# Prologue evictions regrouped by engine, a weight cast and a weight copy moved between engines, and one block's convolution placed one product later

## The chip, the cores and the metric

The kernel runs on one core of a Trainium2 chip. The metric is the device time of one execution in microseconds (us); for a kernel it is the median of several runs. A profiled execution, taken apart from these runs, gives the trace. Engines are named as in the profile: PE is TensorE (matmuls; PEld are its weight loads), DVE is VectorE, ACT is ScalarE, POOL is GpSimd, SP is SyncE, which here only issues DMAs.

## What is computed

The reference, cut to its two parts. `x` is 8 x 3904 x 192, `weight` 8 x 7; `moe_w1` and `moe_w2` are 192 x 1024, `moe_w3` 1024 x 1024, `moe_w_out` 1024 x 192, all float32.

```python
def _attn_ref(x, weight):
    w = softmax(weight, axis=-1)              # 8 heads, 7 taps
    x_pad = np.concatenate([np.zeros((B, 6, D)), x], axis=1)
    idx = np.arange(S)[:, None] + np.arange(7)[None, :]
    x_unf = x_pad[:, idx, :].reshape(B, S, 7, H, D // H)
    return np.einsum('hk,bskhg->bshg', w, x_unf).reshape(B, S, D)

def _moe_ref(x, w1, w2, w3, w_out):           # x: 31232 x 192, from _attn_ref
    a = x @ w1
    b = x @ w2
    return ((a * b) @ w3) @ w_out
```

A causal depthwise convolution of seven taps, a gate that multiplies two products, and two further products.

## The kernel before

**Two streams, rounds and blocks.** The 31232 tokens are two streams of 15616, side by side (`NS` = 2, index `r`). A round `R` is 512 tokens of both streams; there are 31 rounds, worked in groups of four (`GROUP`). The convolution works in windows of 64 rows that give 58 tokens each (`ST`), and windows are gathered in blocks: `SIZES` is 6, 4, 8, 10, 8 and then six blocks of 36 and one of 20. Blocks 0 to 4 make rounds 0 to 3, block 5 makes rounds 4 to 7, and so on.

**Convolution.** `conv` multiplies the windows of x (`xb`, bf16, loaded by POOL's DMAs) with banded 64x64 matrices (`Aband`, made from the taps in the prologue), some heads at a time, into one pair of PSUM banks; the results are evicted to `convo`. One eviction of four heads is two instructions, since the 192 features are stored in three parts of 64 (`NP` = 3, index `k`) and 96 features span one part and a half.

**Transposition to xT.** The products need features on the partitions: `xT[k]`, 64 features of stream 0 over 64 of stream 1, a ring of 2048 tokens. For blocks 0 to 4 TensorE transposes `convo` into PSUM (`pe_transpose`, `joint_transposes`), and an engine evicts it to `xT`. From block 5 on SP stores `convo` to `rows` in DRAM (`store`) and brings it back with transposing DMAs (`transposes`, called by `send`, three for each round). SP's DMAs run in the order in which they are written; a transpose waits for the stores of its rows.

**First product.** For each round and each of eight column tiles `ft` of 128: six matmuls with w1 (three `k`, two streams, 512 columns, the two streams on the upper and lower half of the array) into one pair of banks, six with w2 into another; ScalarE casts the first pair to bf16 (`asb`), VectorE multiplies it with the second into `abT`. Weights lie in `wd[0]` and `wd[1]`, twice each: partitions 0 to 63 for stream 0 and a copy on 64 to 127 for stream 1. They come in four quarters of 256 columns. The first quarter is loaded as float32 (`wfirst`) and cast by four instructions (`cast_w(i, r, engine)`); the others are loaded by POOL with the cast in the DMA (`load_w`) onto the lower half, and copied to the upper half by `copy_w(part, i, engine)`.

**Second product.** `W_sb` is w3 times w_out, made once (`w3_product`) from w3 transposed by DMAs (`w3_transposes`). `second_product(R, r)` multiplies 512 tokens of `abT` with it and sends the output; in the first group POOL issues these outputs, later SP.

**PSUM pairs.** There are four pairs of banks. `banks()` takes the next free one from a list, `drained(p)` puts it back at the end; what a matmul really waits for are the reads of the pair that it gets.

**Order of the work.** The order on each engine is that of the program text (a manual schedule). Prologue: bands and casts, block 0 (L526 to L531), block 1 (L532, L535), the first two column tiles of round 0 in two parts, 348 tokens from block 0 (L534, L536) and 164 from block 1 (L537), then the other six tiles. `first_product` takes a dictionary `between` of what follows a given tile. After rounds 0 to 3 and `w3_product` come the eight second products of the first group; with `at` the convolutions of block 5 (three thirds: heads 0 to 2, 3 to 5, 6 and 7) are placed behind the products 0, 1 and 2, and those of block 6 behind 4, 5 and 6. Block 5's last third is followed by its stores, and `send(7)` sends rounds 4 to 7 to `xT`. Then rounds 4 to 7 are worked, and so on.

Of the kernel before, what the change touches and what calls it, by code (L numbers as in the profile page):

```python
# [16 lines left out]
def kernel(  # L17
# [53 lines left out]
    def banks():  # L71
        p = free.pop(0)
        return p, pairs[:, NS * p:NS * p + NS, :]
# [4 lines left out]
    def drained(p):  # L78
        assert p not in free
        free.append(p)  # L80
# [107 lines left out]
    def cast_w(i, r, f):  # L188
        f(out=wd[i][Q * r:Q * r + Q, :, 0:WC[1]], in_=wfirst[:, i])

    def copy_w(part, i, f):
        cs = slice(WC[part], WC[part + 1])
        f(out=wd[i][Q:128, :, cs], in_=wd[i][0:Q, :, cs])  # L193

    load_w(1)
    cast_w(1, 1, nc.gpsimd.tensor_copy)
    load_w(2)
    load_x(2, between=[seq((copy_w, 1, i, nc.gpsimd.tensor_copy) for i in range(2))])
    load_w(3)
    for i in range(2):  # L200
        copy_w(2, i, nc.gpsimd.tensor_copy)
    load_x(3)

    def warm(n):
# [70 lines left out]
    def conv(b, h0, nh, evict=None):  # L275
        n = SIZES[b] // 2
        if h0 == 0:
            convo_of[b] = work.tile([128, n, NP, NS, Q], BF16, tag="convo", bufs=2, name="convo")
        convo = convo_of[b]
        p, cps = banks()  # L280
        wd = nh * G

        def view(ps, r):
            return cps[ps, r, 0:n * wd].rearrange("p (w g) -> p w g", g=wd)

        for j in range(nh):
            h = h0 + j
            for c in range(2):
                xb, w0 = xb_of[b][c]
                for r in range(NS):  # L290
                    nc.tensor.matmul(  # L291
                        view(slice(Q * c, Q * c + Q), r)[:, :, j * G:(j + 1) * G],
                        band_of(h, r),
                        xb[Q * r:Q * r + Q, w0:w0 + n, h * G:(h + 1) * G],
                        start=True, stop=True)
        src = cps[:, :, 0:n * wd].rearrange("p r (w g) -> p r w g", g=wd)
        o, moves = 0, []
        for k, c0, m in segments(h0 * G, wd):
            moves.append((convo[:, :, k, :, c0:c0 + m].rearrange("p w r g -> p r w g"),
                          src[:, :, :, o:o + m]))  # L300
            o += m
        if h0 + nh == H:
            del xb_of[b]
        if evict == ():
            return p, moves
        if evict == "streams":
            assert nh == H
            return p, [(convo[:, :, :, r, :], src[:, r].rearrange("p w (k g) -> p w k g", k=NP))
                       for r in range(NS)]
        for e, (dst, part) in enumerate(moves):  # L310
            f = evict or [nc.scalar.copy]
            f[e % len(f)](out=dst, in_=part)  # L312
        drained(p)
# [57 lines left out]
    def width(R):  # L371
        return min(CH, TS - R * CH)

    def first_part(R, ft, c0, c1, ks=tuple(range(NP))):
        ab = abT_of[R]
        r0 = (R * CH) % RING
        pq = []
        for i in range(2):
            q, p = banks()
            pq.append((q, p))  # L380
            for k in ks:
                for r in range(NS):
                    rs = slice(Q * r, Q * r + Q)
                    nc.tensor.matmul(  # L384
                        p[:, r, c0:c1], wd[i][rs, k, ft * 128:(ft + 1) * 128],
                        xT[k][rs, r0 + c0:r0 + c1],
                        start=(k == ks[0]), stop=(k == ks[-1]))
        (qa, pa), (qb, pb) = pq
        asb = work.tile([128, NS, CH], BF16, tag="asb", bufs=3, name="asb")
        nc.scalar.copy(out=asb[:, :, c0:c1], in_=pa[:, :, c0:c1])  # L390
        nc.vector.tensor_tensor(out=ab[:, ft, :, c0:c1], in0=asb[:, :, c0:c1],  # L391
                                in1=pb[:, :, c0:c1], op=ALU.mult)
        drained(qa)
        drained(qb)

    def first_rest(R, fts, c0, c1):
        ab = abT_of[R]
        r0 = (R * CH) % RING
        n, ne = c1 - c0, len(fts)
        assert ne * n <= CH  # L400
        pq = []
        for i in range(2):
            q, p = banks()
            pq.append((q, p))
            for e, ft in enumerate(fts):
                for k in range(NP):
                    for r in range(NS):
                        rs = slice(Q * r, Q * r + Q)
                        nc.tensor.matmul(  # L409
                            p[:, r, e * n:e * n + n], wd[i][rs, k, ft * 128:(ft + 1) * 128],  # L410
                            xT[k][rs, r0 + c0:r0 + c1], start=(k == 0), stop=(k == NP - 1))
        (qa, pa), (qb, pb) = pq
        asb = work.tile([128, NS, CH], BF16, tag="asb", bufs=3, name="asb")
        nc.scalar.copy(out=asb[:, :, 0:ne * n], in_=pa[:, :, 0:ne * n])
        a, b = (t[:, :, 0:ne * n].rearrange("p r (e c) -> p r e c", e=ne) for t in (asb, pb))
        nc.vector.tensor_tensor(
            out=ab[:, fts[0]:fts[0] + ne, :, c0:c1].rearrange("p e r c -> p r e c"),
            in0=a, in1=b, op=ALU.mult)
        drained(qa)
        drained(qb)  # L420

    def first_tile(R):
        abT_of[R] = work.tile([128, JT, NS, CH], BF16, tag="abT", bufs=GROUP, name="abT")
# [1 line left out]
    def first_product(R, between=None, fts=range(JT)):  # L425
        if R not in abT_of:
            first_tile(R)
        for ft in fts:
            first_part(R, ft, 0, width(R))
            if between and ft in between:  # L430
                between[ft]()

# [66 lines left out]
    made = [band(1, 0), band(1, 1)]  # L499
    put(V, *made[0])  # L500
    put(V, *made[1])
    cast_w(1, 0, A)

    def move_all(p, moves, fs):
        for f, m in zip(fs, moves):
            move(f, m)
        drained(p)

    def joint_transposes(b):
        n = SIZES[b] // 2  # L510
        assert n * NP <= 2 * CH // 64
        convo = convo_of[b]
        p, tps = banks()
        tps = bf16(tps)
        t0, moves = tok(FIRST[b]), []
        for k in range(NP):
            for w in range(n):
                nc.tensor.transpose(
                    out=tps[:, k * n + w, :],
                    in_=convo[:, w, k].rearrange("p r g -> p (r g)"), identity=ident)  # L520
            src = tps[:, k * n:k * n + n, :].rearrange("p w (c s) -> p c w s", c=2)
            moves.append((xT[k][:, t0:t0 + 2 * n * ST].rearrange("p (c w s) -> p c w s", c=2, w=n),
                          src[:, :, :, 0:ST]))
        return p, moves

    move_all(*conv(0, 0, 4, ()), (V, A))  # L526
    move_all(*conv(0, 4, 4, ()), (A, V))
    for k, f in ((0, A), (2, V), (1, V)):
        p, *m = pe_transpose(0, k)
        move(f, m)  # L530
        drained(p)  # L531
    move_all(*conv(1, 0, H, "streams"), (A, V))  # L532
    first_tile(0)
    first_part(0, 0, 0, EARLY, (0, 2, 1))  # L534
    move_all(*joint_transposes(1), (A, A, V))  # L535
    first_part(0, 1, 0, EARLY)  # L536
    first_rest(0, range(2), EARLY, CH)  # L537
    load_w3(0)
    for i in range(2):
        copy_w(3, i, P)  # L540
# [4 lines left out]
    def need(R):  # L545
        return next(i for i in range(NWIN) if tok(i) >= (R + 1) * CH)

    def send(last):
# [2 lines left out]
            sent[0] += 1  # L551

    first_product(0, {
        4: seq([(conv, 2, 0, 4)]),
        5: seq([(conv, 2, 4, 4)]),
        6: seq([(pe_transposes, 2)]),
# [33 lines left out]
    for p, rounds in enumerate(groups):  # L590
        b = PROLOGUE_BLOCKS + p
        order = rounds[-1:] + rounds[:-1] if rounds[-1] == NR - 1 else rounds
        for j, R in enumerate(order if p else ()):
            first_product(R)
            send(R + GROUP)
            if j < 2 and b < NB:
                P(out=pace, in_=abT_of[R][0:1, JT - 1, 1, 0:2])  # L597
                load_x(b, (j,))
        if b < NB:
            zero(b)  # L600
        at = {1: [(b, slots[0])], 3: [(b, slots[1])], 5: [(b, slots[2])]}
        if p == 0:
            at = {0: [(5, slots[0], (V, A))], 1: [(5, slots[1], (V, A))],
                  2: [(5, slots[2], (V, A), need(GROUP))], 4: at[1], 5: at[3], 6: at[5]}
        for i, (R, r) in enumerate((R, r) for R in rounds for r in range(NS)):
            second_product(R, r, R == NR - 1 and r == 1, nc.sync if p else nc.gpsimd)
            for c in at.get(i, ()) if b < NB else ():
                conv_heads(*c)
            if p == 0 and i == 2:
                send(2 * GROUP - 1)  # L610
    assert sent[0] == NR

# [29 lines left out]
```

## Time and profile before

| what | value |
|---|---|
| median of 3 runs | 524.01 us (523.96 to 524.15) |
| profiled execution, its own time | 523.71 us |
| its span, first to last instruction | 522.0 us |
| mean granted TensorE clock | 0.998 |
| TensorE busy | 514.2 us, 98% of the span |
| VectorE, ScalarE busy | 358.1 us, 326.1 us |
| GpSimd busy | 58.6 us |

The time of the profiled execution is 1.7 us above its span, which lies outside the instructions. A row of the timeline gives the start from the beginning of the span, the duration from the first to the last of a run of like instructions, the engine, the line of the kernel, the operation, output and inputs, the shapes, their number, and in brackets the idle time of the engine before it with what ended it. A q behind an engine's name marks DMA issues. In the table of waits the three numbers are the time in all, the count and the longest. In the chain that ended last each piece has its start, its length and its engine, tile and line.

### The profile page before, as it was taken

How to read it: one execution, taken by the hardware profiler on the slowest of the kernel's cores; microseconds unless marked ns; L12 is line 12 of the kernel's file. 1: busy time of each engine (PE TensorE's matmuls, PEld its weight loads, DVE VectorE, ACT ScalarE, POOL GpSimd, SP SyncE). 2: the span in 40 equal slices, each digit the busy share in tenths (PEclk: the TensorE clock that was granted, in tenths of full speed). 3: DMA queues.
4: the chain of work that ended last, by engine and by line, in shares of the span. 5: the costliest groups of instructions: out<-in, count | busy, mean ns of one | idle time of the engine just before them, and what ended most of it. 6: DMA issues, size and time to landing. Idle time of an engine off the chain costs nothing.

```text
span 522.0 us, 13021 instructions
## 1 busy us (share of the span) xinstructions
PE 514.2 (98%) x5576; PEld 340.5 (65%) x5576; DVE 358.1 (69%) x347; ACT 326.1 (62%) x414; POOL 58.6 (11%) x98
## 2 busy tenths in 40 slices
PE   7999999999999999999999999999999999999997
PEld 4555788444894558845588455884558845599567
DVE  6778646799538995389953899438993299912870
ACT  6887642777437774377743777337774377735762
POOL 8601622030000200003000020001200000000000
PEclk9999999999999999999999999999999999999999
DMA  8979998699556973569645698456824532034004
GB/s 115 157 145 125 148 225 219 161 209 147 129 156 164 111 99 102 152 165 124 86 110 148 158 126 84 118 146 156 102 45 122 153 96 31 17 104 140 1 3 151
DMA packets 133420, 64.61 MB, mean 124 GB/s; under 512 B 90304, under 2 KB 132642, under 8 KB 133298
## 3 DMA queue, kind: packets, MB, share of 16 engines
q1 hardware_dynamic: 94320, 44.06, 35.0%
q0 software_dynamic: 38896, 19.62, 28.8%
q8 instruction: 43, 0.70, 0.6%
q14 instruction: 15, 0.12, 0.1%
q10 hardware_dynamic: 146, 0.10, 0.1%
HBM read 33.25 MB, written 36.52 MB: 134 GB/s over the span
## 4 chain that ended last, share of the span: by engine, by line
PE 90%; issue 3%; DMA 2%; DVE 2%; ACT 1%; POOL 1%; ACTq 0%; POOLq 0%; DVEq 0%
PE pairs L384 56%; PE pairs L445 31%; PE pairs L291 3%; DMA xb<-in_x_dram 2%; DVE abT L391 1%; ACT asb L390 1%; PE pairs L207 1%; POOL xb L120 0%; DVE cprod L248 0%; PE pairs L344 0%; ACT convo L312 0%; DVE convo L489 0%; POOL rows L335 0%; POOL wo_b L567 0%; PE pairs L409 0%
## 5 line engine op out<-in xcount | busy, mean ns | idle before, releaser
L391 DVE TENSOR_TENSOR abT<-asb,pairs 128x1024 bf16<-128x1024 bf16 (+2 forms) x248 | 297.9, 1201 | 76.8 <-ACT asb L390 39.9
L384 PE MATMUL pairs<-xT,wd 64*128 64x512 bf16 (+2 forms) x2976 | 319.4, 372 | 0.8 <-DVE abT L391 0.3
L390 ACT CAST asb<-pairs 128x1024 bf16<-128x1024 f32 (+2 forms) x248 | 247.1, 996 | 67.4 <-PE pairs L384 66.7
L384 PEld LDWEIGHTS <-wd 64*128 64x128 bf16 x2976 | 162.2, 94 | 151.4 <-issue 2.3
L445 PE MATMUL pairs<-W_sb,abT 128*128 128x192 bf16 x1952 | 166.1, 246 | 0.0
L445 PEld LDWEIGHTS <-abT 128*128 128x128 bf16 x1952 | 159.6, 98 | 9.7 <-issue 9.7
L450 ACT COPY osb<-pairs 128x384 f32<-128x384 f32 x122 | 58.3, 478 | 116.0 <-PE pairs L445 116.0
L312 DVE CAST convo<-pairs 128x864 bf16<-128x864 f32 (+5 forms) x67 | 50.8, 815 | 68.5 <-PE pairs L291 64.3
L120 POOL DMA_DIRECT2D xb<-in_x_dram x42 | 32.2, 782 | 6.4 <-PE pairs L384 3.7
L597 POOL COPY pace<-abT 1x2 bf16<-1x2 bf16 x10 | 1.8, 176 | 239.6 <-DVE abT L391 239.6
L291 PE MATMUL pairs<-xb,Aband 64*64 64x432 bf16 (+5 forms) x384 | 17.7, 284 | 0.5 <-POOL xb L575 0.5
L291 PEld LDWEIGHTS <-Aband 64*64 64x64 bf16 x384 | 7.2, 106 | 7.8 <-issue 6.6
L312 ACT CAST convo<-pairs 128x512 bf16<-128x512 f32 (+4 forms) x15 | 8.1, 584 | 1.3 <-PE pairs L291 1.2
L457 POOL DMA_DIRECT2D out_dram<-osb x8 | 6.1, 759 | 18.4 <-ACT osb L450 18.0
L450 DVE COPY osb<-pairs 128x192 f32<-128x192 f32 x1 | 0.4, 357 | 11.1 <-PE pairs L445 11.1
L480 PEld LDWEIGHTS <-w3T 128*128 128x128 bf16 x64 | 5.2, 98 | 0.4 <-issue 0.4
L480 PE MATMUL pairs<-wo_b,w3T 128*128 128x192 bf16 x64 | 5.5, 246 | 0.0
L344 PE MATMUL pairs<-ident,convo 128*128 128x128 bf16 x48 | 3.9, 219 | 1.4 <-DVE convo L489 1.3
L344 PEld LDWEIGHTS <-convo 128*128 128x128 bf16 x48 | 2.9, 97 | 3.2 <-DVE convo L489 1.6
L193 POOL COPY wd<-wd 64x768 bf16<-64x768 bf16 x6 | 4.8, 840 | 0.9 <-DMA wd<-in_moe_w_dram 0.9
L207 PE MATMUL pairs<-zeros 128*128 128x512 bf16 x8 | 3.8, 628 | 1.1 <-DVE ones L155 1.1
L482 ACT CAST W_sb<-pairs 128x192 bf16<-128x192 f32 x8 | 2.6, 319 | 2.8 <-PE pairs L480 2.8
(56 smaller groups left out, 42.0 us busy)
## 6 DMA issues: line engine op xcount, KB each, us to landing
out_dram<-osb SPq DMA_DIRECT2D x52, 384.0 KB
xb<-in_x_dram POOLq DMA_DIRECT2D x18, 432.0 KB, 7.5
rows<-convo SPq DMA_DIRECT2D x8, 648.0 KB
out_dram<-osb POOLq DMA_DIRECT2D x8, 384.0 KB, 4.8
w3rows<-in_moe_w_dram POOLq DMA_DIRECT2D x2, 1024.0 KB, 11.7
xb<-in_x_dram POOLq DMA_DIRECT2D x6, 240.0 KB, 5.3
rows<-convo SPq DMA_DIRECT2D x4, 324.0 KB
xT<-rows SPq DMA_TRANSPOSE x81
```

The lines of the kernel that those rows point to most:

```text
L120: nc.gpsimd.dma_start(out=xb[Q * r:Q * r + Q, w:w + m, :], in_=x_spans(r, i, m))
L207: nc.tensor.matmul(t[:, j % 2, :], zeros, zeros[:, 0:1].to_broadcast([128, CH]), start=True, stop=True)
L291: nc.tensor.matmul(view(slice(Q * c, Q * c + Q), r)[:, :, j * G:(j + 1) * G], band_of(h, r), xb[Q * r:Q * r + Q, w0:w0 + n, h * G:(h + 1) ...
L312: f[e % len(f)](out=dst, in_=part)
L344: nc.tensor.transpose(out=tps[:, w, :], in_=convo[:, w, k].rearrange("p r g -> p (r g)"), identity=ident)
L384: nc.tensor.matmul(p[:, r, c0:c1], wd[i][rs, k, ft * 128:(ft + 1) * 128], xT[k][rs, r0 + c0:r0 + c1], start=(k == ks[0]), stop=(k == ks[-1]))
L390: nc.scalar.copy(out=asb[:, :, c0:c1], in_=pa[:, :, c0:c1])
L391: nc.vector.tensor_tensor(out=ab[:, ft, :, c0:c1], in0=asb[:, :, c0:c1], in1=pb[:, :, c0:c1], op=ALU.mult)
L445: nc.tensor.matmul(ops[:, (g - g0) * D:(g - g0) * D + D], ab[:, jt, r, g * 128:(g + 1) * 128], W_sb[:, jt, :], start=(jt == 0), stop=(jt = ...
L450: f(out=osb[:, g0:g0 + per, :].rearrange("p g d -> p (g d)"), in_=ops[:, 0:per * D])
L457: queue.dma_start(out=out[t0:t0 + ng * 128, :].rearrange("(g p) d -> p g d", p=128), in_=osb)
L480: nc.tensor.matmul(wps[:, 0, 0:D], w3T[:, gt, jt * 128:(jt + 1) * 128], wo_b[:, gt, :], start=(gt == 0), stop=(gt == JT - 1))
```

## The change

Five edits, all but the last in the prologue.

1. Block 0: `conv(0, 0, 4)` is evicted by VectorE alone and `conv(0, 4, 4)` by ScalarE alone; before, each pair was shared by both. The three transposes come in the order 0, 1, 2 and are evicted by VectorE, VectorE, ScalarE (before: 0, 2, 1 by ScalarE, VectorE, VectorE). The product follows the order 0, 1, 2 too.
2. The cast of the second weight's first quarter for stream 0 moves from ScalarE to POOL, which now makes both; POOL makes only one copy of the third quarter, and ScalarE makes the other behind column tile 2 of round 0.
3. `first_part` and `first_rest` become three functions, `first_factor` (matmuls of one weight), `first_cast` and `first_times`. The two parts of tiles 0 and 1 are interleaved anew: factor of w1, its cast, the convolution of block 1, factor of w2, and the same around the joint transposes. The bank pair of the w1 factor goes back to the list right after the cast.
4. In `joint_transposes` the third part goes to the second bank of the pair (slots 0, 2 and 8 in place of 0, 2 and 4); block 1's two streams are evicted by VectorE and ScalarE, before by ScalarE and VectorE.
5. The thirds of block 5's convolution stand behind the second products 1, 2 and 3, and `send(7)` behind product 3.

```diff
     load_w(1)
-    cast_w(1, 1, nc.gpsimd.tensor_copy)
+    for r in range(NS):
+        cast_w(1, r, nc.gpsimd.tensor_copy)
     load_w(2)
     load_x(2, between=[seq((copy_w, 1, i, nc.gpsimd.tensor_copy) for i in range(2))])
     load_w(3)
-    for i in range(2):
-        copy_w(2, i, nc.gpsimd.tensor_copy)
+    copy_w(2, 1, nc.gpsimd.tensor_copy)
     load_x(3)
...
+    def first_factor(R, i, fts, c0, c1):
+        n, r0 = c1 - c0, (R * CH) % RING
+        q, p = banks()
+        for e, ft in enumerate(fts):
+            for k in range(NP):
+                for r in range(NS):
+                    rs = slice(Q * r, Q * r + Q)
+                    nc.tensor.matmul(
+                        p[:, r, e * n:e * n + n], wd[i][rs, k, ft * 128:(ft + 1) * 128],
+                        xT[k][rs, r0 + c0:r0 + c1], start=(k == 0), stop=(k == NP - 1))
+        return q, p[:, :, 0:len(fts) * n]
+
+    def first_cast(qa, pa):
+        asb = work.tile([128, NS, CH], BF16, tag="asb", bufs=3, name="asb")
+        asb = asb[:, :, 0:pa.shape[2]]
+        nc.scalar.copy(out=asb, in_=pa)
+        drained(qa)
+        return asb
+
+    def first_times(R, fts, c0, c1, asb, qb, pb):
...
+        nc.vector.tensor_tensor(out=dst, in0=asb, in1=pb, op=ALU.mult)
+        drained(qb)
...
+    def first_part(R, fts, c0, c1):
+        a, b = (first_factor(R, i, fts, c0, c1) for i in range(2))
+        first_times(R, fts, c0, c1, first_cast(*a), *b)
...
-    cast_w(1, 0, A)
...
+        B2 = CH // 64
+        at = [0, n, B2]
...
-    move_all(*conv(0, 0, 4, ()), (V, A))
-    move_all(*conv(0, 4, 4, ()), (A, V))
-    for k, f in ((0, A), (2, V), (1, V)):
+    move_all(*conv(0, 0, 4, ()), (V, V))
+    move_all(*conv(0, 4, 4, ()), (A, A))
+    for k, f in enumerate((V, V, A)):
         p, *m = pe_transpose(0, k)
         move(f, m)
         drained(p)
-    move_all(*conv(1, 0, H, "streams"), (A, V))
     first_tile(0)
-    first_part(0, 0, 0, EARLY, (0, 2, 1))
+    a0 = first_factor(0, 0, [0], 0, EARLY)
+    c0 = first_cast(*a0)
+    move_all(*conv(1, 0, H, "streams"), (V, A))
+    b0 = first_factor(0, 1, [0], 0, EARLY)
+    first_times(0, [0], 0, EARLY, c0, *b0)
+    a1 = first_factor(0, 0, [1], 0, EARLY)
+    c1 = first_cast(*a1)
     move_all(*joint_transposes(1), (A, A, V))
-    first_part(0, 1, 0, EARLY)
-    first_rest(0, range(2), EARLY, CH)
+    b1 = first_factor(0, 1, [1], 0, EARLY)
+    first_times(0, [1], 0, EARLY, c1, *b1)
+    first_part(0, [0, 1], EARLY, CH)
...
     first_product(0, {
+        2: seq([(copy_w, 2, 0, A)]),
         4: seq([(conv, 2, 0, 4)]),
...
         if p == 0:
-            at = {0: [(5, slots[0], (V, A))], 1: [(5, slots[1], (V, A))],
-                  2: [(5, slots[2], (V, A), need(GROUP))], 4: at[1], 5: at[3], 6: at[5]}
+            at = {1: [(5, slots[0], (V, A))], 2: [(5, slots[1], (V, A))],
+                  3: [(5, slots[2], (V, A), need(GROUP))], 4: at[1], 5: at[3], 6: at[5]}
...
-            if p == 0 and i == 2:
+            if p == 0 and i == 3:
                 send(2 * GROUP - 1)
```

More of the change, by code (lines that the diff above doesn't have):

```diff
@@ L372, in width @@
         return min(CH, TS - R * CH)
[L374 to L381, printed above, removed]
+    def first_factor(R, i, fts, c0, c1):
+        n, r0 = c1 - c0, (R * CH) % RING
+        assert len(fts) * n <= CH
+        q, p = banks()
+        for e, ft in enumerate(fts):
+            for k in range(NP):
                 for r in range(NS):
@@ L384, in first_part @@
                     nc.tensor.matmul(
[L385 to L388, printed above, removed]
+                        p[:, r, e * n:e * n + n], wd[i][rs, k, ft * 128:(ft + 1) * 128],
+                        xT[k][rs, r0 + c0:r0 + c1], start=(k == 0), stop=(k == NP - 1))
+        return q, p[:, :, 0:len(fts) * n]
+    def first_cast(qa, pa):
@@ L389, in first_part @@
         asb = work.tile([128, NS, CH], BF16, tag="asb", bufs=3, name="asb")
-        nc.scalar.copy(out=asb[:, :, c0:c1], in_=pa[:, :, c0:c1])
-        nc.vector.tensor_tensor(out=ab[:, ft, :, c0:c1], in0=asb[:, :, c0:c1],
-                                in1=pb[:, :, c0:c1], op=ALU.mult)
+        asb = asb[:, :, 0:pa.shape[2]]
+        nc.scalar.copy(out=asb, in_=pa)
         drained(qa)
-        drained(qb)
[L396 to L420, printed above, removed]
@@ new lines, in first_cast @@
+        return asb
+    def first_times(R, fts, c0, c1, asb, qb, pb):
+        ab, ne = abT_of[R], len(fts)
+        if ne == 1:
+            dst = ab[:, fts[0], :, c0:c1]
+        else:
+            dst = ab[:, fts[0]:fts[0] + ne, :, c0:c1].rearrange("p e r c -> p r e c")
+            asb, pb = (t.rearrange("p r (e c) -> p r e c", e=ne) for t in (asb, pb))
+        nc.vector.tensor_tensor(out=dst, in0=asb, in1=pb, op=ALU.mult)
+        drained(qb)
+    def first_part(R, fts, c0, c1):
+        a, b = (first_factor(R, i, fts, c0, c1) for i in range(2))
+        first_times(R, fts, c0, c1, first_cast(*a), *b)
@@ L428, in first_product @@
         for ft in fts:
-            first_part(R, ft, 0, width(R))
+            first_part(R, [ft], 0, width(R))
             if between and ft in between:
@@ L510, in joint_transposes @@
         n = SIZES[b] // 2
-        assert n * NP <= 2 * CH // 64
+        B2 = CH // 64
+        at = [0, n, B2]
+        assert 2 * n <= B2
         convo = convo_of[b]
@@ L518, in joint_transposes @@
                 nc.tensor.transpose(
-                    out=tps[:, k * n + w, :],
+                    out=tps[:, at[k] + w, :],
                     in_=convo[:, w, k].rearrange("p r g -> p (r g)"), identity=ident)
-            src = tps[:, k * n:k * n + n, :].rearrange("p w (c s) -> p c w s", c=2)
+            src = tps[:, at[k]:at[k] + n, :].rearrange("p w (c s) -> p c w s", c=2)
             moves.append((xT[k][:, t0:t0 + 2 * n * ST].rearrange("p (c w s) -> p c w s", c=2, w=n),
```

## The prediction

> **What bounds the kernel now.** I read the page first, then TensorE's waits, then the timeline at the two places where the change works, and the chain that ended last. In the page, span and busy times:
>
> ```profile
> span 522.0 us, 13021 instructions
> ...
> PE 514.2 (98%) x5576; PEld 340.5 (65%) x5576; DVE 358.1 (69%) x347; ACT 326.1 (62%) x414; POOL 58.6 (11%) x98
> ```
>
> TensorE is idle for 7.8 us in all, so only a change of that idle time, or of the time that TensorE spends half-fed, can show. Its waits (times in total, count, longest) are few:
>
> ```profile
> PE pairs L344 <- DVE convo L489: 1.3, 2, 0.8
> ...
> PE pairs L291 <- POOL xb L575: 0.5, 2, 0.4
> ```
>
> The first is the prologue, the second the convolution of block 5. The change works on both. After the prologue the chain is TensorE's own work nearly to the end, so a delay there is paid in full and not regained. By 0.2% I mean 1.05 us, about what a measurement of this kernel can tell from no change.
>
> **Part 1: evictions of block 0, the cast that leaves ScalarE, the order of the prologue.** The timeline of before (start, duration, engine, line):
>
> ```profile
> 6.88 0.71 PE L291 MATMUL pairs<-xb,Aband 64*64 64x72 bf16 x32
> ...
> 7.15 0.82 POOL L189 CAST wd<-wfirst 64x768 bf16<-64x768 f32 x1
> 7.43 0.56 DVE L489 CAST convo<-pairs 128x384 bf16<-128x384 f32 x1 [0.15 <-PE pairs L291]
> ...
> 8.03 0.54 ACT L489 CAST convo<-pairs 128x192 bf16<-128x192 f32 x2
> ...
> 8.45 0.47 ACT L489 COPY xT<-pairs 128x348 bf16<-128x348 bf16 x1
> 8.60 0.56 DVE L489 CAST convo<-pairs 128x384 bf16<-128x384 f32 x1 [0.61 <-ACT convo L489]
> ...
> 9.59 0.58 DVE L489 COPY xT<-pairs 128x348 bf16<-128x348 bf16 x2 [0.44 <-PE pairs L344]
> ...
> 9.65 0.44 PE L291 MATMUL pairs<-xb,Aband 64*64 64x48 bf16 x32
> ...
> 10.02 1.06 PE L384 MATMUL pairs<-xT,wd 64*128 64x348 bf16 x12
> 10.14 0.48 ACT L489 CAST convo<-pairs 128x384 bf16<-128x384 f32 x1 [1.22 <-PE pairs L291]
> ...
> 10.68 0.74 ACT L390 CAST asb<-pairs 128x696 bf16<-128x696 f32 x1
> 10.77 1.59 POOL L193 COPY wd<-wd 64x768 bf16<-64x768 bf16 x2 [0.86 <-DMA wd<-in_moe_w_dram]
> ...
> 11.01 0.51 PE L518 MATMUL pairs<-ident,convo 128*128 128x128 bf16 x6
> ...
> 11.56 0.61 ACT L489 COPY xT<-pairs 128x232 bf16<-128x232 bf16 x2
> ...
> 12.39 1.07 PE L409 MATMUL pairs<-xT,wd 64*128 64x164 bf16 x24
> ...
> 13.28 4.07 PE L384 MATMUL pairs<-xT,wd 64*128 64x512 bf16 x36
> ```
>
> VectorE's second eviction stood at 8.60 behind ScalarE's two reads of the same banks, which themselves began late (8.03) behind a weight cast. With one engine for each pair: VectorE evicts the first pair from 7.43 (0.56 + about 0.3, an estimate from ScalarE's 0.27 for each of its two of that size) to 8.3; ScalarE, rid of the cast, the second from 7.65 (0.27 + 0.48) to 8.4. The transposes then go at 8.05, 8.3 and 8.5 instead of 8.05 and 9.21; xT is out at 8.8 and 9.05 (VectorE, 0.58 for two) and 9.4 (ScalarE, 0.47), and the first half product (six matmuls, about 0.5) ends its issue at 9.55. In before the last xT came at 10.17: 0.8 us is won here.
>
> It does not last. TensorE goes on with the convolution of block 1 (0.3), the other half product (0.45; its weights are ready, POOL's two casts at 0.82 end by 8.8) and the next first half, to 10.85. The joint transposes now need ScalarE's half of block 1's eviction, and that stands behind the new early cast of asb: 9.8 to 10.5, then 0.48, so 10.95. They start at 11.0, as in before (11.01). What is left of the win is that one half product (0.45) is done before them and not after. Behind them ScalarE has the second cast of asb (11.05 to 11.8) ahead of its two evictions of xT (0.61 for both, out at 12.1 and 12.4). The joined product therefore starts at 12.1 instead of 12.39, waits 0.2 at its second step, and lasts 0.89 (13.28 − 12.39): full width starts at 13.2 against 13.28. **Won: 0.1 us.**
>
> POOL's queue: its second cast (0.82) goes ahead of the third weight quarter's loads, a load of x and the copies of the second quarter; POOL idled 0.86 us ahead of those copies for a load to land, so they stay at 10.77. Later POOL is rid of one copy, and the loads of block 3 and of w3 go out 0.8 us earlier: no cost.
>
> **Part 2: the copy that goes to ScalarE** (third weight quarter, 64x768 bf16), between the casts of the third and fourth column tile of round 0. No row shows ScalarE copying bf16 within SBUF. The nearest is its weight cast of the same size:
>
> ```profile
> L189 ACT CAST wd<-wfirst 64x768 bf16<-64x768 f32 x3 | 2.5, 831 | 1.5 <-DMA wfirst<-in_moe_w_dram 1.4
> ```
>
> I take 0.83; the bounds are 0.48 (ScalarE's eviction of 384 elements a partition, above) and 1.02 (its cast of 1024, below). What is queued behind it on ScalarE is on the path. The chain of before:
>
> ```profile
> 15.44 1.02 ACT asb L390
> 16.48 1.23 DVE abT L391
> 17.75 1.47 PE pairs L384 x12
> ```
>
> The cast of the fourth tile, VectorE's product of it, and TensorE's sixth tile, which waits for those banks. In the changed kernel the third tile's cast runs 14.1 to 15.1, the copy to 15.9, so the fourth's cast starts at 15.9 instead of 15.44, VectorE at 16.9, TensorE at 18.15 instead of 17.75. The fifth tile, whose weights the copy makes, starts 0.1 late, inside that. **Lost against before, with the 0.1 won counted: +0.4 us** (bounds +0.1 and +0.55). Nothing behind it gives this back: TensorE had no slack there.
>
> **Part 3: block 5's convolution one second product later.** The timeline:
>
> ```profile
> 67.58 0.37 PE L291 MATMUL pairs<-xb,Aband 64*64 64x432 bf16 x2
> ...
> 68.52 0.25 POOL L575 MEMSET xb<- 6x192 bf16 x1 [0.26 <-DMA xb<-in_x_dram]
> ...
> 69.46 2.81 PE L445 MATMUL pairs<-W_sb,abT 128*128 128x192 bf16 x32
> ...
> 72.20 0.74 PE L291 MATMUL pairs<-xb,Aband 64*64 64x432 bf16 x12
> ...
> 72.88 2.81 PE L445 MATMUL pairs<-W_sb,abT 128*128 128x192 bf16 x32
> ```
>
> The first third took 67.58 to 69.46, 1.88 us; the second, with x there, 72.20 to 72.88, 0.68. So **1.2 us** were lost to x, which is complete at 68.8. In the changed kernel TensorE comes there at 67.58 + 0.4 + 2.74 (a second product: 72.20 − 69.46) = 70.7. The wait goes whole.
>
> What is late next is round 5's xT: SP stores block 5's rows and then transposes them back from DRAM, and all of this hangs on the last third of block 5.
>
> ```profile
> 51.09 1.26 SPq L474 DMA_TRANSPOSE w3T<-w3rows  x1
> ...
> 53.86 0.18 POOL L568 COPY pace<-w3T 1x2 bf16<-1x2 bf16 x1 [12.02 <-DMA w3T<-w3rows]
> ...
> 76.26 0.88 ACT L312 CAST convo<-pairs 128x864 bf16<-128x864 f32 x1
> ...
> 77.17 0.91 SPq L335 DMA_DIRECT2D rows<-convo  x2
> ...
> 82.36 4.05 SPq L364 DMA_TRANSPOSE xT<-rows  x3
> ...
> 86.46 4.57 SPq L335 DMA_DIRECT2D rows<-convo  x4
> ...
> 96.42 3.74 SPq L364 DMA_TRANSPOSE xT<-rows  x3
> ```
>
> and of the chain, one group of four rounds:
>
> ```profile
> 91.64 41.55 PE pairs L384 x384
> ```
>
> The first transposes of xT are round 4, the last ones round 5. A transpose landed 2.75 us after its issue (51.09 to 53.86 for the w3T that POOL waits for), so round 5's third lands at about 96.42 + 3.74 − 1.26 + 2.75 = 101.65. TensorE begins round 4 at 91.6 and needs 41.55 / 4 = 10.4 for a round; it needs that third xT two steps of 0.21 into round 5, at 102.4. The margin is 0.75 us. Now the last third of block 5 ends 1.9 us later (0.4 + 2.74 − 1.2), while TensorE's need comes 0.8 us earlier (0.4 − 1.2). With a chain of the same length TensorE waits 1.9 + 0.8 − 0.75 = 1.95 us. Round 4's own xT is in by 82.36 + 4.05 − 1.2 + 2.75 = 88.0; its margin to the need at 92.0 is 4.0, of which 1.9 + 0.8 = 2.7 go.
>
> The chain need not keep its length. Its first store took 77.17 to 82.36, 5.2 us, which I put down to what POOL had issued before and was still draining, block 6's x and the first outputs:
>
> ```profile
> 78.00:82.00 4.00, 1.00 0.91 253
> ```
>
> ```profile
> rows<-convo SPq DMA_DIRECT2D x4, 324.0 KB
> ...
> rows<-convo POOLq DMA_DIRECT2D x1, 36.0 KB, 2.0
> ```
>
> The first is a window of time (its bounds, length, granted clock, DMA share, GB/s), the others DMA issues (size, us to landing). The DMA engines were 0.91 busy at 253 GB/s. A store of this kind with 36 KB landed in 2.0 us; 324 KB and its small second part at about 200 GB/s add some 1.9, so 3.9 without company. At 79.0 the new store meets one output transfer and no x. The chain can be 0 to 1.3 us shorter; I take 1.1, nearer to the empty case, as x is gone by then. **The new wait: 0.85 us** (bounds 0.6 and 1.95; 0 if the later stores speed up too). The Trainium skill, "DMA: Bandwidth & Descriptors", Queues, rings and completion order, says that each DMA engine turns between the queues packet by packet, so an output that is in flight still takes its share from the store: by that page alone the chain is hardly shorter and the sum 1 us higher, which is the first rival.
>
> **Sum**, against the profiled execution's 523.71 us (span 522.0): +0.4 − 1.2 + 0.85 = +0.05. The median of before is 524.01, 0.3 above the profiled one, and goes the same way: **524.0 us**, no change to be measured.
>
> **Rivals.**
> (a) Slower: the store chain keeps its 24.5 us (77.17 to 101.65), since one of POOL's outputs is in flight at each of its stages as before. Then TensorE waits 1.95 us at round 5, and the sum is +0.4 − 1.2 + 1.95 = +1.15, with the dearer copy +1.3: 525.2. It decides once the first store takes 5 us or more. For it: the 0.91 leaves the engines little room. Against: x is gone by then.
> (b) The chain shortens by 1.9 or more, in the later stores too, for one output fewer is left behind it. Next to no wait at round 5, 0.2 left: 0.4 − 1.2 + 0.2 = −0.6, 523.4. For it: outputs and stores share the same engines at 253 GB/s. Against: SP's own issue time (3.74 for three transposes) does not shrink.
> (c) The prologue keeps its win of 0.8, because the casts of asb and the copy find room on ScalarE that I don't see (it is busy for 62% of the span). Then −0.5 (0.8 won, 0.3 of it spent on the copy) stands in place of +0.4: the sum is −0.5 − 1.2 + 0.85 = −0.85, and −1.5 where (b) holds too; between them 522.8. Against: every step behind 11.0 waits for ScalarE in my order of it.
> (d) The moved convolution does not lose its wait, because x is late too: POOL's order ahead of x changes. Then 1.2 comes back, 525.2. Against: 1.9 us of margin.
>
> **How the numbers follow.** Forecast 0.40, (a) 0.20, (b) 0.20, (c) 0.15, (d) 0.05. Faster by over 0.2%: most of (c) and the edges of (b) and of the forecast, 0.20. Slower: (a) and (d), 0.25. Within: 0.55. The range leaves out the far end of (c) and what lies above (a): 522.7 to 525.4.
>
> **What would show it.** Right: ScalarE's 64x768 copy of about 0.83 us ahead of the fourth cast of 1024 columns; TensorE's sixth tile of round 0 at about 18.1; no wait of L291 for the POOL memset; round 4 beginning near 90.8; a TensorE wait for xT of 0.6 to 1.2 us near 101, the first ever for that tile. Wrong: round 0's full width starting before 12.8 (c), no wait near 101 (b), or one near 2 us (a).

## The result, and the profile after

| | before | after |
|---|---|---|
| median | 523.96 us (522.50 to 524.16) | **525.48 us** (524.79 to 528.42) |
| ratio, 95% interval | | 1.0041 (1.0027 to 1.0055) |
| profiled execution, its own time | 523.71 us | 528.42 us |

The change makes the kernel 1.5 us slower, well beyond its uncertainty. 524.0 was predicted, within 522.7 to 525.4; rival (a) stood at 525.2. The profiled execution is the longest of the twelve of after, so it shows the loss enlarged; a second profile (`e11_after_again`, 524.73 us) stands below beside it.

TensorE's waits of after, total, count and longest:

```profile
PE pairs L382 <- DMA xT<-rows: 2.9, 4, 0.9
...
PE pairs L382 <- DVE abT L401: 0.8, 3, 0.5
```

Of the two old waits, L291's for x is gone and L344's is down from 1.3 to 0.6. TensorE now waits for xT, which it never did before, and longer for VectorE in round 0 (0.8 us against 0.3). The timeline of after at the two places, first round 0 (start, duration, engine, line):

```profile
14.29 1.01 ACT L390 CAST asb<-pairs 128x1024 bf16<-128x1024 f32 x1 [0.41 <-PE pairs L382]
...
15.32 0.83 ACT L193 COPY wd<-wd 64x768 bf16<-64x768 bf16 x1
...
16.18 1.93 ACT L390 CAST asb<-pairs 128x1024 bf16<-128x1024 f32 x2
...
17.22 2.35 DVE L401 TENSOR_TENSOR abT<-asb,pairs 128x1024 bf16<-128x1024 bf16 x2 [0.67 <-ACT asb L390]
...
18.49 1.47 PE L382 MATMUL pairs<-xT,wd 64*128 64x512 bf16 x12 [0.53 <-DVE abT L401]
```

The copy takes 0.83 on ScalarE, as predicted, and pushes the fourth cast, its product and TensorE's sixth tile: 18.49 where before had 17.75. (0.14 of this lies ahead of the change's work: block 0's transposes start at 8.19 here and at 8.05 in before. Counted from them, the sixth tile is 0.60 later.) Then block 5 and rounds 4 and 5:

```profile
67.33 0.25 POOL L569 MEMSET xb<- 6x192 bf16 x1 [0.30 <-DMA xb<-in_x_dram]
...
70.99 0.74 PE L291 MATMUL pairs<-xb,Aband 64*64 64x432 bf16 x12
...
79.38 0.89 SPq L335 DMA_DIRECT2D rows<-convo  x2
...
84.94 3.92 SPq L364 DMA_TRANSPOSE xT<-rows  x3
...
91.14 0.60 PE L382 MATMUL pairs<-xT,wd 64*128 64x512 bf16 x4
...
92.08 10.11 PE L382 MATMUL pairs<-xT,wd 64*128 64x512 bf16 x92 [0.34 <-DMA xT<-rows]
...
100.27 13.96 SPq L364 DMA_TRANSPOSE xT<-rows  x9
...
102.90 0.39 PE L382 MATMUL pairs<-xT,wd 64*128 64x512 bf16 x2 [0.72 <-DMA xT<-rows]
...
104.22 0.39 PE L382 MATMUL pairs<-xT,wd 64*128 64x512 bf16 x2 [0.93 <-DMA xT<-rows]
...
105.51 6.71 PE L382 MATMUL pairs<-xT,wd 64*128 64x512 bf16 x46 [0.89 <-DMA xT<-rows]
```

x is complete at 67.6 and TensorE comes at 71.0: no wait. The first store takes 79.38 to 84.94, **5.56 us**, not the 3.9 to 4.1 that the forecast needs; this is the point at which rival (a) said it decides. The transposes of round 5 leave SP at 100.27, 20.9 behind the first store (before: 19.25), and TensorE waits for each of the three xT in turn, 2.54 in all, after 0.34 already at round 4. A wait in brackets is counted from the modelled end of the matmul ahead of it; counted by the pace of two matmuls in 0.21, each wait costs some 0.2 more, an estimate from these rows (0.39 for two).

The windows of after (bounds, length, busy time of PE, PEld, DVE, ACT and POOL, then the granted clock, DMA share, GB/s) show what came on top in this execution:

```profile
100.00:104.00 4.00, 2.58 (x24) 1.11 (x20) 3.67 (x3) 2.02 (x2) 0.03 (x1) 1.00 0.38 86
104.00:106.00 2.00, 0.89 (x6) 0.34 (x7) 0.00 (x0) 0.00 (x0) 1.63 (x3) 0.83 0.53 121
106.00:108.00 2.00, 2.00 (x12) 0.77 (x10) 0.49 (x1) 1.01 (x1) 0.24 (x1) 0.50 0.92 86
108.00:110.00 2.00, 2.00 (x18) 1.00 (x16) 0.97 (x2) 1.01 (x1) 0.00 (x0) 0.82 2.07 190
```

Behind the waits TensorE's granted clock falls to 0.50, so 2 us hold 12 matmuls and not 22 as in before. That part seems not to be in most executions: ten of the twelve have a mean clock of 0.998 or more and lie at 524.8 to 526.4.

### The profile page after: what moved, and what is told of

It is laid out like the page before. It is cut to its first block, busy times and chain, and to the rows that moved or that the text cites. A ratio compares the mean times of both kernels' runs of the same rounds, so it can differ in the third digit from the quotient of the medians.

```text
span 526.7 us, 13019 instructions
## 1 busy us (share of the span) xinstructions
PE 517.0 (98%) x5576; PEld 342.9 (65%) x5576; DVE 357.9 (68%) x347; ACT 325.9 (62%) x414; POOL 58.5 (11%) x98
## 4 chain that ended last, share of the span: by engine, by line
PE 95%; ACT 1%; DVE 1%; DMA 1%; issue 0%; SPq 0%; ACTq 0%; DVEq 0%
PE pairs L382 59%; PE pairs L431 31%; PE pairs L291 3%; DMA xT<-rows 1%; DVE abT L401 1%; ACT asb L390 1%; PE pairs L466 1%; PE pairs L207 1%; PE pairs L344 1%; PE pairs L257 0%; ACT convo L312 0%; DVE convo L475 0%; ACT xT L356 0%; SPq L364 0%; ACT xT L475 0%
## 5 line engine op out<-in xcount | busy, mean ns | idle before, releaser
L382 PE MATMUL pairs<-xT,wd 64*128 64x512 bf16 (+3 forms) x3000 | 323.4, 372 | 4.2 <-DMA xT<-rows 2.9
L382 PEld LDWEIGHTS <-wd 64*128 64x128 bf16 x3000 | 165.3, 94 | 155.9 <-issue 9.0
L291 PE MATMUL pairs<-xb,Aband 64*64 64x432 bf16 (+5 forms) x384 | 16.9, 284 | 0.1
L291 PEld LDWEIGHTS <-Aband 64*64 64x64 bf16 x384 | 6.9, 106 | 7.0 <-issue 6.2
L344 PE MATMUL pairs<-ident,convo 128*128 128x128 bf16 x48 | 3.9, 219 | 0.7 <-DVE convo L475 0.6
L344 PEld LDWEIGHTS <-convo 128*128 128x128 bf16 x48 | 2.9, 97 | 2.5 <-issue 1.5
```

The lines of the kernel that those rows point to most:

```text
L291: nc.tensor.matmul(view(slice(Q * c, Q * c + Q), r)[:, :, j * G:(j + 1) * G], band_of(h, r), xb[Q * r:Q * r + Q, w0:w0 + n, h * G:(h + 1) ...
L344: nc.tensor.transpose(out=tps[:, w, :], in_=convo[:, w, k].rearrange("p r g -> p (r g)"), identity=ident)
L382: nc.tensor.matmul(p[:, r, e * n:e * n + n], wd[i][rs, k, ft * 128:(ft + 1) * 128], xT[k][rs, r0 + c0:r0 + c1], start=(k == 0), stop=(k == ...
```

## Experiments

Four questions. Is it the move of block 5 (edit 5) or the prologue (edits 1 to 4)? If the move, is the wait for xT there because POOL's outputs share the DMA engines with the stores (contention), or because round 5's transposes stand behind the stores of the second half (order)? Does the prologue's copy cost what was predicted? And why does before itself spread from 522.5 to 526.4? The median of before beside these runs was 523.97 to 524.01.

**`e1_move_only`**: before with edit 5 alone.

```diff
-            at = {0: [(5, slots[0], (V, A))], 1: [(5, slots[1], (V, A))],
-                  2: [(5, slots[2], (V, A), need(GROUP))], 4: at[1], 5: at[3], 6: at[5]}
+            at = {1: [(5, slots[0], (V, A))], 2: [(5, slots[1], (V, A))],
+                  3: [(5, slots[2], (V, A), need(GROUP))], 4: at[1], 5: at[3], 6: at[5]}
...
-            if p == 0 and i == 2:
+            if p == 0 and i == 3:
```

> The kernel before with the move of block 5's thirds alone (edit 5). Theory CHAIN (the loss is TensorE's wait for round 5's xT, because block 5's stores and transposes now end too late): the 1.2 us of waiting for x goes, the last third ends 1.5 us later, TensorE comes 1.2 us earlier, and against the old margin of 0.75 a wait of 2 to 3 us for xT appears; 0.8 to 1.8 us slower than before, and the wait near 102. Theory PROLOGUE (the loss is made ahead of round 1, the move is a gain): 1.2 us faster than before, no wait for xT.

Measured: 526.37 us (525.28 to 527.74), ratio 1.005 (1.003 to 1.007). The move alone makes the kernel slower, by 2.40 us, more than the whole change does and more than the 0.8 to 1.8 that CHAIN gave it.

**`e2_prologue_only`**: after with edit 5 undone (the same lines, the other way round).

> The changed kernel with block 5's thirds back behind the second products 0, 1 and 2 (edits 1 to 4 alone). CHAIN: no wait for round 5's xT; the prologue costs 0.4 to 0.7, and because POOL issues w3 and then x earlier (x was there 1.2 us earlier in the changed kernel's trace), the wait for x shrinks from 1.2 to 0.0 to 0.4; 0.2 to 0.8 us faster than before. PROLOGUE: about 1.5 slower than before.

Measured: 523.23 us (523.06 to 523.39), ratio 0.9989 (0.9977 to 1.0002). So the move costs 525.48 − 523.23 = **2.25 us**; edits 1 to 4 take 0.7 off the median, where +0.4 was predicted (the interval of this ratio just reaches no change, as before itself spreads). The timeline of this kernel shows that there was no wait for x to be won either:

```profile
65.16 0.25 POOL L569 MEMSET xb<- 6x192 bf16 x1 [0.19 <-DMA xb<-in_x_dram]
...
68.45 0.74 PE L291 MATMUL pairs<-xb,Aband 64*64 64x432 bf16 x12
...
91.24 18.95 PE L382 MATMUL pairs<-xT,wd 64*128 64x512 bf16 x174
```

Block 5's first third comes at 68.45 without the move, x is complete at 65.4, and rounds 4 and 5 run through without a wait.

**`e6_after_without_four_outputs`**: after without the DMAs that send the results of the second products 3 to 6 (that part of the output is left out), all else as it is.

```diff
-        if not last:
+        if not last and not (queue is nc.gpsimd and 3 <= NS * R + r <= 6):
```

> The changed kernel without the DMAs that send the outputs of the second products 3, 4, 5 and 6 (that part of the output is left out), which are in flight while block 5 is stored. CONTENTION (the outputs slow the stores): the stores and transposes get 2 to 4 us shorter, no wait for xT, 522.9 to 523.6. LENGTH (SP's stores and transposes take their 19 to 21 us by themselves, and just begin too late): the wait stays and it is 525 or more.

Measured: 523.21 us (523.03 to 523.36), ratio 0.9985 (0.9975 to 0.9996). Its timeline:

```profile
79.46 0.86 SPq L335 DMA_DIRECT2D rows<-convo  x2
...
83.29 3.73 SPq L364 DMA_TRANSPOSE xT<-rows  x3
...
91.22 18.95 PE L382 MATMUL pairs<-xT,wd 64*128 64x512 bf16 x174
...
94.28 12.72 SPq L364 DMA_TRANSPOSE xT<-rows  x9
```

The store takes 3.83 us (the prediction's 3.9 "without company" was right), the whole chain from the first store to round 5's transposes 14.8 and not 20.9, and the wait for xT is gone. The DMA view of 78 to 86 us says who the company is: q0 is POOL's queue, q1 SP's (packets, MB, share of 16 engines). In after:

```profile
q0 software_dynamic: 261, 0.85, 32.0%
q1 hardware_dynamic: 548, 0.40, 23.8%
```

and without the four outputs:

```profile
q1 hardware_dynamic: 1159, 0.55, 31.8%
q0 software_dynamic: 12, 0.04, 1.2%
```

With POOL's 0.85 MB in the way SP moves 0.40 MB in this time, without it 0.55 MB, and sooner. In after an output leaves POOL at 75.29, 78.70, 81.94 and 85.36, one for each second product, and lands 4.2, 3.3, 4.1 and 3.6 us later: from issue to landing there is always at least one on its way, and the store of 79.38 meets the second and the third. That the outputs lengthen the store and the chain is shown; how the two queues share an engine is not. This kernel is also as fast as `e2`, so apart from the outputs the move neither costs nor gains.

**`e4_round5_sent_early`**: after with round 5's transposes right behind the first half of the stores.

```diff
-                store(b, last=first), send(NR), store(b, first))
+                store(b, last=first), send(NR), store(b, first, FIRST[b] + SIZES[b] // 2),
+                send(NR), store(b, FIRST[b] + SIZES[b] // 2))
```

> The changed kernel with round 5's three transposes issued on SP right behind the stores of the first half of block 5 that hold its rows, ahead of the stores of the second half; nothing else differs. CHAIN, where SP's order is what makes round 5 late: its transposes go some 7 us earlier, the wait for xT goes, and 0.5 to 0.9 us faster than before (523.2). Rival CONTENTION (the DMA engines, busy with outputs, make every store late whatever the order): the wait stays above 1 us and the kernel stays 1 us or more slower than before.

Measured: 525.19 us (524.65 to 526.00), ratio 1.0028 (1.0015 to 1.0042); 0.3 below after, within the spread of both. Round 5's transposes do leave earlier, and the chain of waits shows where the loss went:

```profile
87.37 4.30 DMA xT<-rows
...
106.81 7.11 DMA xT<-rows
```

The first piece is round 4's xT, the second now round 6's. Another order on SP only chooses which round is late: the order as the cause falls, and CONTENTION's expectation (a wait above 1 us, 1 us or more slower than before) holds with 1.4 and 1.22.

**`e7_thirds_behind_1_2_2`**: after with the last third, the stores and `send(7)` behind product 2, so that the stores start earlier but the first third as late as in after.

```diff
-            at = {1: [(5, slots[0], (V, A))], 2: [(5, slots[1], (V, A))],
-                  3: [(5, slots[2], (V, A), need(GROUP))], 4: at[1], 5: at[3], 6: at[5]}
+            at = {1: [(5, slots[0], (V, A))],
+                  2: [(5, slots[1], (V, A)), (5, slots[2], (V, A), need(GROUP))],
+                  4: at[1], 5: at[3], 6: at[5]}
```

> The changed kernel with the last third of block 5 placed right behind the second, after second product 2 and not 3, and its sends with it; the first third stays behind product 1. CHAIN (the wait is set by when the last third ends): it ends 2.7 us earlier, the waits for xT go, and apart from up to 1 us in which TensorE waits for free banks at the five heads in a row the time is that of edits 1 to 4 alone: 523.2 to 524.2. If something else of the move costs: 525 or more.

Measured: 523.75 us (523.67 to 525.79), ratio 0.9995 (0.9979 to 1.0011), 0.5 above `e2`. The first store leaves at 77.77 and no xT is waited for, but five heads in a row run out of PSUM banks, a new wait in its list:

```profile
PE pairs L291 <- DVE convo L312: 0.5, 1, 0.5
```

This run holds a second test of contention, with all outputs sent. Its store is as short as in `e6`:

```profile
77.77 0.87 SPq L335 DMA_DIRECT2D rows<-convo  x2
...
79.70 0.75 POOL L443 DMA_DIRECT2D out_dram<-osb  x1 [3.84 <-ACT osb L436]
...
81.68 4.03 SPq L364 DMA_TRANSPOSE xT<-rows  x3
```

3.91 us: the output ahead of it left POOL at 75.11 and landed 3.6 later, and the five heads in a row put the next one off to 79.70, nearly 2 us into the store. In after the next output left 0.7 ahead of the store.

**`e3_prologue_pool_copies`** and **`e5_prologue_dve_copy`**: `e2` with the copy taken off ScalarE. In `e3` POOL makes both, as before; in `e5` VectorE makes one ahead of the third column tile's product.

```diff
 # e3
-    copy_w(2, 1, nc.gpsimd.tensor_copy)
+    for i in range(2):
+        copy_w(2, i, nc.gpsimd.tensor_copy)
...
-        2: seq([(copy_w, 2, 0, A)]),
 # e5
+    copy_w(2, 0, V)
...
-        2: seq([(copy_w, 2, 0, A)]),
```

> As the run before it, and both copies of the third weight quarter on POOL again, none on ScalarE. If the copy on ScalarE is what costs (both theories say 0.45): the prologue is 0.1 faster than before at the sixth tile of round 0 in place of 0.4 slower. If POOL's lost copy is what brings x earlier, x comes about as late as before and 1 us of its wait returns: then about as before, within 0.4. If x is early for another reason: 1.0 to 1.3 faster than before.

> Edits 1 to 4 without the move, and the copy of the third weight quarter made by VectorE ahead of its third product, where it idled 0.6 us, in place of ScalarE. If ScalarE's copy is what holds up the fourth cast: 0.3 to 0.6 us faster than edits 1 to 4 alone (523.2), so 522.6 to 522.9, and the sixth tile of round 0 starts about 0.6 earlier. If the prologue's cost lies elsewhere: 523.2 as there.

Measured: `e3` 523.03 us (522.45 to 524.55), ratio 0.9987 (0.9973 to 1.0000), its spread too wide to tell the copy's price. `e5` **522.54 us** (522.49 to 523.00), ratio 0.9975 (0.9963 to 0.9987), the fastest kernel of the study and faster than both, a little below the range expected. Its timeline:

```profile
14.64 0.66 DVE L193 COPY wd<-wd 64x768 bf16<-64x768 bf16 x1
...
17.74 1.47 PE L382 MATMUL pairs<-xT,wd 64*128 64x512 bf16 x12
```

VectorE ends the copy at 15.30, 0.14 behind the cast that the third product needs, which does not reach TensorE: the sixth tile comes at 17.74, without the wait for VectorE. By the medians ScalarE's copy costs 523.23 − 522.54 = 0.69 us. The traces agree. From block 0's transposes to the sixth tile it is 10.30 in after (8.19 to 18.49), 9.68 in `e5` (8.06 to 17.74), 9.66 in `e3` (8.16 to 17.82) and 9.70 in before (8.05 to 17.75).

**`e8_before_gaps_filled`**: before with five dummy matmuls in the two gaps of TensorE around block 0's transposes.

```diff
+    warm(2)
     for k, f in ((0, A), (2, V), (1, V)):
         p, *m = pe_transpose(0, k)
         move(f, m)
         drained(p)
+        if k == 0:
+            warm(3)
```

> The kernel before with five dummy matmuls (results not used) in the two gaps of the prologue in which TensorE waits for block 0's evictions: two ahead of the first transposes, three behind them. CLOCK (the times of before fall in three groups, 522.5 at a mean granted clock of 0.999, 524.0 at 0.996, 525.3 at 0.993, because the clock is halved for some us after those gaps in some executions): nearly all executions come at 0.998 or more, median 522.5 to 522.9. If the groups have another cause: the median stays near 524.0 and the groups remain.

Measured: 522.94 us (522.75 to 523.28), ratio 0.9977 (0.9967 to 0.9987), the mean clock 0.999 or more in all twelve. The schedule won nothing (from block 0's transposes to the sixth tile 9.70 us, as in the first profile of before), and the median fell by 1.07 us: what was won is the granted clock, and the spread fell from 4 us to 0.5. The clock is not all of before's spread: 4 of its 12 executions at 0.998 or more still took 523.7 to 524.7 us. The wait for x, 1.2 in the first profile (523.71), may be in some of them, but these executions have no trace.

**`e9_before_again`**, **`e10_before_once_more`** and **`e11_after_again`**: the two kernels unchanged, to see what of a profile belongs to one execution.

> The kernel before, unchanged, one more profiled execution. Theory CLOCK and X-VARIES: the granted clock of the prologue's slices between 10 and 14 us is a matter of the execution, so a run with a mean clock of 0.999 or more is at 522.5 to 523.2 us with that stretch at full clock, and one of 0.998 or less is at 523.8 to 525 with about half clock there; the end of the second memset of block 5's x falls anywhere from 66 to 69 us, so the convolution's wait for it is anywhere from 0 to 1.2. Rival FIXED: both repeat the first profile, the wait 1.2 and x complete at 68.8 within 0.2.

> The same kernel before again. X-VARIES expects an end of that memset which differs from the other executions' by 0.5 us or more, and a convolution wait that differs with it; FIXED expects 68.8 and 1.2 again.

> The changed kernel, unchanged, one more profiled execution. CONTENTION expects the wait for round 5's xT again, 1.5 to 3 us in all, a first store of 5 us or more, and 524.8 to 526.5 us; the part of the first profile's 528.4 that is beyond this was TensorE's clock after the waits, and the slices at 104 to 110 us are then at 0.9 or more here. Rival: the slow slices belong to the change whatever the execution, and 528 comes again.

Measured: 522.72, 523.99 and 524.73 us. In both of before's the second memset of x ends at 67.6 and 67.0, ahead of TensorE (67.80 and 69.06): the wait of 1.2 is in neither. `e10` has another loss in its place. Its two gaps around the transposes, and its windows:

```profile
8.04 0.34 PE L344 MATMUL pairs<-ident,convo 128*128 128x128 bf16 x3 [0.34 <-DVE convo L489]
...
9.20 0.51 PE L344 MATMUL pairs<-ident,convo 128*128 128x128 bf16 x6 [0.82 <-DVE convo L489]
```

```profile
8.00:10.00 2.00, 1.14 (x41) 0.84 (x41) 0.97 (x3) 0.91 (x4) 1.87 (x3) 1.00 0.85 98
10.00:12.00 2.00, 2.00 (x28) 1.03 (x17) 0.86 (x3) 1.22 (x2) 1.18 (x2) 0.56 1.14 128
12.00:14.00 2.00, 2.00 (x21) 1.15 (x21) 1.02 (x2) 1.07 (x3) 2.00 (x4) 0.59 0.49 55
```

Behind 2 us in which TensorE worked for 1.14, its clock is 0.56 and 0.59 for 4 us, and full width starts at 14.77 instead of 13.28 in the first profile of before, 1.5 later. In `e9`, and in the first profile of before, the same slices are at 1.00. The mean clock alone does not sort the executions quite as its expectation had it (`e9` has 0.998 and 522.72). After's second profile has the wait for xT and no slow clock behind it:

```profile
79.20 0.91 SPq L335 DMA_DIRECT2D rows<-convo  x2
...
85.03 3.76 SPq L364 DMA_TRANSPOSE xT<-rows  x3
...
98.11 13.40 SPq L364 DMA_TRANSPOSE xT<-rows  x9
...
103.38 6.87 PE L382 MATMUL pairs<-xT,wd 64*128 64x512 bf16 x62 [0.90 <-DMA xT<-rows]
```

The first store takes 5.83, the wait is 0.90, with about 0.4 more at round 4 (its next matmuls start at 91.80, by the pace they were due at 91.4); both together are less than the 1.5 expected, and this execution is also faster than all twelve of the result. So the enlarged loss of the first profile (528.42) is that execution's: slower stores behind the first one (88.9 to 100.3 against 88.8 to 98.1) and the clock.

## Why the prediction was wrong, step by step

The move was forecast at −1.2 + 0.85 = −0.35 and cost 2.25 by the medians of after and `e2` (2.40 by `e1`). Of the 2.6 between them 1.2 is the wait for x, and about 1.4 the wait for xT.

**The new wait (0.85, "I take 1.1 shorter"): wrong, the largest miss.** The chain from the first store to round 5's transposes was 18.9 (`e11`) and 20.9 (the first profile) in after and 18.8 in `e1`; in the seven profiles without the move it was 18.8 to 19.4. It did not get 1.1 shorter in any of them, and TensorE waited at round 5 for 0.90 to 2.54. The prediction read the DMA share of 0.91 in before as one pool that x and the output fill together, and concluded that with x gone the store runs nearly free. But the outputs are enough: the store took 5.56 and 5.83 us with outputs and no x, 3.83 without outputs, and 3.91 in `e7`, where the next output came late. The Trainium skill, "DMA: Bandwidth & Descriptors", Queues, rings and completion order, says that engines turn between queues packet by packet; the longer store agrees with that, the packets themselves no run here shows. Rival (a) had this mechanism. That its 525.2 is 0.3 from the median is in part luck, since its sum also holds the −1.2 for x and the +0.4, and by the medians the runs have 0 and −0.7 in their place.

**Round 4's margin ("2.75 from issue to landing", 1.3 left): wrong.** The 2.75 came from transposes at 51 us, when SP's queue was the only one that moved data. Behind the second products the last transpose of round 4 took 4.2 to 4.4 by the chains of after, `e11` and `e4` (87.37 4.30 above), and TensorE waited 0.34 there in the first profile of after. At round 5, with the outputs done, the figure holds: 2.7.

**The wait for x (−1.2): wrong in size.** The timeline was read rightly, for one execution. Over the thirteen profiles of these kernels the second memset of x ends anywhere between 65.4 and 68.8, and TensorE comes there at 67.6 to 69.1 without the move; 1.2 is the far end. `e6` has the move, no outputs beside the stores and the time of `e2`, so this term is about 0. With it fell the only gain that the prediction saw in the move.

**The prologue (+0.4): the mechanism right, step for step, and 0.2 too cheap.** The joint transposes at 11.0 as in before, the copy of 0.83, the fourth cast late: in `e11` the copy runs from 15.15, the cast from 16.00, the sixth tile from 18.32, forecast for 15.1, 15.9 and 18.15. Counted from block 0's transposes the cost is 0.60. The copy alone is 0.62 of it by the traces of after and `e5` (0.69 by the medians of `e2` and `e5`), where the prediction had about 0.5 (+0.4 with 0.1 won ahead of it). Rival (c) did not come: without the copy the schedule of `e5` is 0.02 ahead of before, so nothing of the 0.8 was kept.

**What the prediction did not have: the clock.** Edit 1 closes the second of TensorE's two gaps in the prologue, the one of 0.82, and leaves the first (0.43 to 0.61 in after, `e2`, `e5` and `e11`). The order of work gains next to nothing by it, as predicted, but the slow clock that most executions of before have afterwards is gone: all 12 executions of `e2`, and of `e5`, have a mean clock of 0.998 or more. `e5`, which has edits 1 to 4 without ScalarE's copy, lies 1.47 below the median of before. `e8`, where only the clock changed, lies 1.07 below it; what the other 0.4 is, no run here separates.

The parts by the runs: −1.47 (edits 1 to 4 without the copy) + 0.69 (copy) + 2.25 (move) = +1.47; measured 525.48 − 523.96 = +1.52. These parts are differences along one row of kernels, so they must add up; the independent figures are `e1`'s 2.40 for the move, `e8`'s 1.07 for the clock and the 0.62 of the traces for the copy. The forecast's near zero also rested on a coincidence: the profiled execution of before had full clock and a wait of 1.2 for x; `e10` has no such wait and loses 1.5 by the clock. Both give about 524, and by the mean clock (23 of 35 executions at 0.997 or less) the second kind is the usual one. That the usual one has no wait for x is seen in `e10` alone, and not shown for the rest.

## What to carry to other kernels

In this kernel a DMA chain on one queue took the length that its neighbours on other queues left it; to cost a store, find out which transfer is in flight beside it at the new time, and don't expect that fewer neighbours help as long as one large one stays. A wait on a load that the profile shows once is one sample of a time that wanders by microseconds: before building on it, look whether a second execution has it. And short idle gaps of TensorE can cost more than their length, so work that is moved into such gaps may pay even where the schedule behind it shows no gain (`e8`: 1.07 us).

## What the runs showed of the hardware that was not expected

The granted TensorE clock can fall to about half for some us behind gaps of less than a microsecond that follow each other closely: 0.34 and 0.82 us with transposes in between (`e10`, clock 0.56 and 0.59 for 4 us), 0.72, 0.93 and 0.89 (after, 0.83, 0.50 and 0.82 over 6 us). Behind a single wait of 0.90 (`e11`) or 1.00 (`e1`) at the same place it stayed at 1.00. It happens in part of the executions of the same kernel: of 35 runs of before, 23 had a mean clock of 0.997 or less, at 523.8 to 526.4 us, and 12 one of 0.998 or more, at 522.5 to 524.7 (`e9` has such gaps, 0.61 and 0.82, and full clock there). Filling the gaps with five dummy matmuls ended it (`e8`). The Trainium skill, "TensorE: Matmul & The Clock Gate", HAM oscillation — how this bites in real kernels, warns of idle gaps above about 3.4 us; these gaps are far shorter (0.82 in `e10`), and here the measurement decides. The Trainium skill, "TensorE: Matmul & The Clock Gate", Part 1: The HAM clock gate (the "warmup" mystery), also says that the window in which activity is judged runs freely and is not tied to the kernel's start, which agrees with the same gaps being punished in one execution and not in the next (`e10`, `e9`).

A 64x768 bf16 copy within SBUF took 0.83 us on ScalarE, as its cast from float32 does, and 0.66 on VectorE. By the chains above, the landing of a transposing DMA for which TensorE waited came 2.7 us after its issue at round 5, 4.2 to 4.4 at round 4 beside the outputs, and 7.1 at round 6 in `e4`, where the packets of POOL's queue, loads of x, took 94% of the time of the 16 engines over 106 to 114 us.
